# The expert phase of an attention, MLP and mixture-of-experts kernel: lists loaded at a tile's begin, weights asked for behind the branch on the count, raw buffers refilled behind each conversion

## The chip, the cores and the metric

The kernel runs on one core of a Trainium2 chip. The metric is the device time of one execution in microseconds (us), as the median of several runs. A core has five engines that run their own instruction streams: TensorE (PE, matrix products), VectorE (DVE), ScalarE (ACT), GpSimd (POOL) and SyncE (SP, which here only asks for DMA transfers). They meet through semaphores.

## The reference, cut to what matters

```python
def _moe2_ref(x, w_gate, w1, w2):            # x: 2304 x 512, from attention and an MLP ahead of it
    logits = x @ w_gate                      # 8 experts
    expert_idx = np.argmax(logits, axis=1)
    probs = softmax(logits)
    gate_w = probs[np.arange(N), expert_idx]
    for e in range(E):
        mask = expert_idx == e
        if not mask.any():
            continue
        xe = x[mask]
        h = np.maximum(xe @ w1[e], 0.0)      # 512 -> 1024
        ye = h @ w2[e]                       # 1024 -> 512
        out[mask] = gate_w[mask, None] * ye
```

Attention (4 batches, 8 heads, 576 positions of 64) gives x, an MLP with 2048 hidden units follows, and then this expert phase. How many tokens an expert gets is known only when the gate has been computed. With the inputs shown the experts, sorted by size, have 1366, 515, 296, 103 and 24 tokens; the other three have none.

## The kernel before, in words

Attention and the MLP run to about 640 us of the span; a planner orders their instructions, and the change leaves that part alone. The expert phase (`run`, from L1185 on) takes the experts in order of size, r = 0, 1, 2, ... For each of them the tokens' numbers and gate weights stand in a list in DRAM (`info`, two 32-bit words for each token).

**Tiles.** An expert's tokens are cut into tiles of 256 (`tile256`), and what is left runs as a tile of 128 or 64 (`tile128`, `tile64`, in `remainder`); an expert with 128 tokens or fewer has only such a tile (`only`). So expert 0 has five tiles of 256 and one of 128, expert 1 two and one of 64, expert 2 one and one of 64, expert 3 one of 128, expert 4 one of 64. Tile j of expert r is called (r, j) here.

**Steps of a tile.** `fetch` loads the list of 256 tokens into `it` (a DMA of SP, L1020), copies it into `rem` for the remainder (L1024), and gathers the tokens' rows from DRAM into `xg`, in two halves of 128 rows (indirect DMAs of POOL, L1026). `xprep` transposes a half on TensorE (`Tx`, L1033); ScalarE and VectorE split it into a high and a low part (`cxh` L1035, `cxl` L1036). Then come two layers of three-pass products (L1060; L1143 in `tile64`), and a scatter of the scaled rows to the output (POOL, L1064).

**Weights.** The 16 weight blocks of an expert (256 KB each) are loaded by SP into 16 `raw` buffers (`wload`, L1004), and each is then split by `conv` (ScalarE L1014, VectorE L1015) into the tiles `e` that TensorE reads. The conversions of expert r+1 are `jobs`, handed out by `step` between the products of a tile of expert r; `ahead` holds the steps that prepare the next tile. `load_next`, called behind a tile that has conversions, asks for the blocks of expert r+2 in the 16 buffers.

**Branches.** All five engines follow the branches on the counts. `few0` (L1295) and `many0` (L1302) branch on the size of expert 0, `less{r}` (L1313) and `more{r}` (L1317) on that of expert r; L1316 leaves the loop when nothing is left (in the trace it has the line of the loop's frame, L1307). `hint` (L1199) marks a place where an engine is told which way a labelled branch will go, so that the instructions there can be fetched ahead. An engine that jumps over a part adds what that part would have added to its semaphores; the trace has this as EVENT_SEMAPHORE and, for POOL, INC_SWDGE_SEM at the branch's line.

**Order around the change.** Tile (0, 0) runs ahead of the branch `few0`. Its `ahead` (L1286) holds, in this order, the counts, the 16 loads for expert 1, and the two transposes of tile (0, 1), whose gather is issued in the same tile. SP issues in program order, so what stands behind the 16 loads on its stream comes later.

Of the kernel before, what the change touches and what calls it, by code (L numbers as in the profile page):

```python
# [10 lines left out]
I32 = mybir.dt.int32  # L11
# [945 lines left out]
class Experts:  # L957
# [7 lines left out]
    def __init__(A, tc, K, wp, cp, psp, x2, info, w1, w2, out):  # L965
# [5 lines left out]
        A.its = [[cp.tile([P, 2, 2], I32, name=f"it{z}{q}") for q in range(2)] for z in range(2)]  # L971
# [8 lines left out]
    def itile(A, r, j):  # L980
        return A.its[0][r % 2] if j == 0 else A.its[1][j % 2]
# [35 lines left out]
    def fetch(A, r, j, base, rows=NT + 1):  # L1017
# [5 lines left out]
        if j:  # L1023
            A.nc.sync.dma_start(A.rem, src)  # L1024
        for h in range(2):
            A.nc.gpsimd.indirect_dma_start(out=A.xg[:, h], out_offset=None, in_=A.x2[0:rows, :], in_offset=IOA(ap=it[:, h, 0:1], axis=0))  # L1026
# [13 lines left out]
    def body(A, r, j, size, jobs=(), ahead=(), at={}, it=None, cond=None):  # L1040
# [13 lines left out]
        {2 * P: A.tile256, P: A.tile128, 64: A.tile64}[size](name, A.Ws[r % 2], A.itile(r, j) if it is None else it, A.xtile(j), step)  # L1054
# [40 lines left out]
    def tile128(A, n, W, it, x, step):  # L1095
# [22 lines left out]
        step(5)  # L1118
        l1(0, range(4))
        step(3)  # L1120
        l1(1, (0, 1))
        turn(0)
        step(2)
# [4 lines left out]
        step(7, 2)  # L1128
# [4 lines left out]
    def tile64(A, n, W, it, x, step):  # L1133
# [23 lines left out]
        def l2(h, fs):  # L1157
# [5 lines left out]
            if f == 7:  # L1163
                nc.scalar.mul(yo[0:64, c], Y[h][64:128], it[64:128, 0, 1:2].bitcast(F32))
                nc.vector.scalar_tensor_tensor(yo[0:64, c], Y[h][0:64], it[0:64, 0, 1:2].bitcast(F32), yo[0:64, c], op0=ALU.mult, op1=ALU.add)

        nc.sync.dma_start(it[64:128, 0], it[0:64, 0])
# [17 lines left out]
    def run(A, base, last, order, order_all):  # L1185
# [15 lines left out]
        def nexts(r, j, b, nb):  # L1201
            fs = [lambda: None] + xpreps(r, j) if b is not None else []
            if nb is not None:
                fs += [lambda: A.fetch(r + 1, 0, nb)]
                fs += [lambda: None] * (6 - len(fs)) + xpreps(r + 1, 0)
            return fs

        def load_next(r):
            if r < E - 2:
                A.load_raws(r + 2, reg(0, r + 2, E - 1))  # L1210

        def big(r, j, b, jobs=(), nb=None):
# [4 lines left out]
            if more:  # L1217
                A.fetch(r, j + 1, b)
            A.body(r, j, 2 * P, jobs, nexts(r, j + 1, b if more else None, nb))
            if jobs:  # L1220
                load_next(r)
# [31 lines left out]

        def only(r, nb):

            jobs = [lambda: A.fetch(r + 1, 0, nb)] + [lambda i=i: A.conv(r + 1, i) for i in range(16)] if r < E - 1 else []
            if r < E - 2:
                jobs[-1] = lambda: (A.conv(r + 1, 15), load_next(r))

            def go(size):  # L1260
                hint(f"more{r}", ns[r] > P)
                A.body(r, 0, size, jobs, xpreps(r + 1, 0) if jobs else (), cond=ns[r + 1] > 0 if jobs else None)

            with A.tc.If(ns[r] <= 64) as c:  # L1264
# [21 lines left out]
        ahead = [lambda: None] * 2 + [counts, lambda: A.load_raws(1, hold["e1"]), lambda: None] + xpreps(0, 1)  # L1286
# [230 lines left out]
```

## Time and profile before

| | |
|---|---|
| median of 3 runs | 927.5 us (924.5, 927.5, 933.88) |
| the profiled execution | 926.22 us, span 924.5 us |
| PE busy | 869.6 us (94% of the span) |
| DVE, ACT, POOL busy | 560.1, 401.7, 314.3 us |
| mean granted TensorE clock | 0.987 of full speed |

TensorE is busy nearly throughout. The idle time before an instruction is shown in a row with what ended it: an engine's instruction, a DMA, or an engine's sequencer (a name with q, as DVEq: a branch or a semaphore event of that stream). "issue" is time for which the profile shows no releaser. The rows that the prediction uses stand in a section of their own below.

### The profile page before, as it was taken

The page shows a single profiled execution, that of the slowest core. Times are in us where ns is not written, and L with a number is a line of the kernel's source. Part 1 is how long each engine was busy: PE and PEld are TensorE (multiplying, and loading weights), DVE is VectorE, ACT ScalarE, POOL GpSimd, SP SyncE. Part 2 cuts the span into 40 slices and gives each one's busy share as a digit, 9 for nine tenths or more (in the row PEclk, how much of TensorE's full clock was granted, in tenths as well). Part 3 has the DMA queues.
Part 4 walks back from the last instruction along what each step waited for, and adds up shares of the span by engine and source line. Part 5 has one row for each costly group of instructions (what it writes and reads, how often), then busy time and mean ns, then how long its engine had stood idle before and what let it go on. Part 6 is the DMA issues. An engine that isn't in the chain of part 4 may idle for free. (4 is left out here: it accounts for less than half of the span.)

```text
span 924.5 us, 17837 instructions
## 1 busy us (share of the span) xinstructions
PE 869.6 (94%) x6185; PEld 740.4 (80%) x6185; DVE 560.1 (61%) x1387; ACT 401.7 (43%) x1022; POOL 314.3 (34%) x332
## 2 busy tenths in 40 slices
PE   7998989999999999999999999999899998998883
PEld 6665657888888888888889989899788987888763
DVE  4999986757677767877756666556226211613450
ACT  6777765545445545555422121223225222523451
POOL 1555665433344354453342232341212111111110
PEclk9999989999999999999999999999999999999997
DMA  9982101323232133312111131153527212612561
GB/s 336 357 303 93 40 6 36 90 64 95 101 94 96 57 101 102 111 35 74 59 54 69 62 76 52 41 124 106 187 78 229 70 48 62 212 50 83 174 192 38
DMA packets 49724, 98.39 MB, mean 106 GB/s; under 512 B 12575, under 2 KB 19375, under 8 KB 49584
## 3 DMA queue, kind: packets, MB, share of 16 engines
q1 hardware_dynamic: 38720, 76.78, 25.6%
q0 software_dynamic: 4240, 11.56, 4.0%
q10 hardware_dynamic: 6624, 8.39, 2.6%
q8 instruction: 63, 1.03, 0.5%
q14 instruction: 77, 0.63, 0.2%
HBM read 83.43 MB, written 13.67 MB: 105 GB/s over the span
## 5 line engine op out<-in xcount | busy, mean ns | idle before, releaser
L707 PE MATMUL l<-xh,wi 128*128 128x256 f32 x1024 | 205.4, 285 | 1.4 <-DVE t L686 1.4
L707 PEld LDWEIGHTS l<-xh,wi 128*128 128x128 f32 x1024 | 166.7, 190 | 6.1 <-DVE t L686 1.8
L737 PE MATMUL acc<-wo,gh 128*128 128x512 f32 x512 | 166.0, 405 | 0.0
L707 PE MATMUL l<-xl,wi 128*128 128x256 f32 x512 | 144.6, 282 | 0.0
L713 POOL TENSOR_TENSOR gl<-t,gh 128x256 fp32r<-128x256 f32 x107 | 82.0, 766 | 180.3 <-ACT gh L710 149.7
L530 POOL TENSOR_SCALAR P<-P,sm 128x256 f32<-128x256 f32 (+4 forms) x71 | 88.3, 1250 | 101.5 <-ACT gh L710 46.5
L710 ACT CAST gh<-t 128x256 fp32r<-128x256 f32 x120 | 48.8, 406 | 170.2 <-DVE t L686 99.3
L685 DVE TENSOR_SCALAR t<-l,al 128x256 f32<-128x256 f32 x128 | 61.8, 483 | 86.9 <-PE l L707 84.8
L737 PE MATMUL acc<-wo,gl 128*128 128x512 f32 x256 | 100.5, 393 | 1.2 <-POOL gl L713 1.2
L707 PEld LDWEIGHTS l<-xl,wi 128*128 128x128 f32 x512 | 97.4, 190 | 3.8 <-issue 0.2
L737 PEld LDWEIGHTS acc<-wo,gh 128*128 128x128 f32 x512 | 86.6, 189 | 10.8 <-issue 0.5
L479 DVE TENSOR_REDUCE nb<-S 128x1 f32<-128x256 f32 (+4 forms) x160 | 69.5, 476 | 29.6 <-PE S L456 14.9
L524 ACT COPY F<-PT 128x384 f32<-128x384 f32 (+2 forms) x126 | 58.5, 479 | 64.2 <-PE PT L519 60.8
L823 DVE SCALAR_TENSOR_TENSOR xt<-y,xr_wg 128x512 f32<-128x512 f32 x96 | 73.8, 769 | 9.1 <-DMA xr_wg<-in_wgT_dram 5.2
L519 PE MATMUL PT<-ident,P 128*128 128x128 f32 (+1 forms) x400 | 64.9, 282 | 7.4 <-DVE xo L573 5.3
L496 ACT ACTIVATE P<-S,nb 128x128 f32<-128x128 f32 (+3 forms) x128 | 66.7, 529 | 9.3 <-DVE nb L479 8.5
L519 PEld LDWEIGHTS PT<-ident,P 128*128 128x128 f32 (+1 forms) x400 | 45.5, 140 | 21.1 <-DVE xo L573 5.0
L1060 PE MATMUL l<-cxh,e 128*128 128x256 f32 x320 | 58.2, 282 | 0.8 <-ACTq L1295 0.8
L737 PEld LDWEIGHTS acc<-wo,gl 128*128 128x128 f32 x256 | 48.1, 188 | 13.0 <-POOL gl L713 2.1
L686 DVE SCALAR_TENSOR_TENSOR t<-l,t 128x256 f32<-128x256 f32 x128 | 54.4, 425 | 4.4
L1060 PE MATMUL Y<-e,hh 128*128 128x512 f32 x176 | 56.2, 400 | 0.0
L1015 DVE TENSOR_TENSOR e<-raw,e 128x512 fp32r<-128x512 f32 x68 | 43.9, 685 | 19.5 <-ACT e L1014 19.3
(375 smaller groups left out, 1683.3 us busy)
## 6 DMA issues: line engine op xcount, KB each, us to landing
raw<-in_moe_w_dram SPq DMA_DIRECT2D x96, 256.0 KB, 4.2
xr_wg<-in_wgT_dram SPq DMA_DIRECT2D x24, 512.0 KB, 3.6
qk<-in_qk_dram SPq DMA_DIRECT2D x16, 608.0 KB, 3.9
rawi<-in_moe_w_in_dram SPq DMA_DIRECT2D x16, 512.0 KB, 8.8
rawo<-in_moe_w_out_dram SPq DMA_DIRECT2D x16, 512.0 KB, 10.6
v<-in_v_dram SPq DMA_DIRECT2D x16, 320.0 KB, 3.1
x<-y ACTq DMA_DIRECT2D x16, 256.0 KB, 3.3
xr<-xT SPq DMA_DIRECT2D x7, 512.0 KB
```

The costliest lines, as they stand in the source:

```text
L479: nc.vector.tensor_reduce(pl["nb", p, c][:, 2 * k + j:2 * k + j + 1], pl[Ss[j]][:, a:b], axis=AX.X, op=ALU.max, negate=True)
L496: nc.scalar.activation(pl[x][:, a:b], pl[Ss[j]][:, a:b], AF.Exp, bias=nb, scale=1.0, accum_out=pl["sm", p, c][:, 2 * k + j:2 * k + j + 1])
L519: nc.tensor.transpose(pl[t][0:w, k], pl[x][:, P * k:P * k + w], A.K.ident)
L524: f(pl[F][:, 0:n], pl[t][:, 0:n])
L530: (nc.gpsimd if on == "POOL" else nc.vector).tensor_scalar(y, y, pl["sm", p, c][:, k:k + 1], None, op0=ALU.mult)
L685: nc.vector.tensor_scalar(pl[out], x, 0.0, A.K.al[:, f:f + 1], op0=ALU.min, op1=ALU.mult)
L686: nc.vector.scalar_tensor_tensor(pl[out], x, 0.0, pl[out], op0=ALU.max, op1=ALU.add)
L707: nc.tensor.matmul(pl[l][:, 0:G], lhsT=a[:, c], rhs=b, start=k == 0 and j == 0, stop=k == 3 and j == 2)
L713: (nc.gpsimd if on == "POOL" else nc.vector).tensor_sub(pl[gl], pl[t], pl[gh].bitcast(F32))
L737: nc.tensor.matmul(pl[acc], lhsT=x[:, c], rhs=w, start=f == 0 and j == 0, stop=f == 15 and j == 2)
L823: A.nc.vector.scalar_tensor_tensor(t, A.y(i), 1.0, wg, op0=ALU.mult, op1=ALU.mult, accum_out=A.L()[:, i, e:e + 1])
L1060: A.nc.tensor.matmul(ps, lhsT=x[a], rhs=w[b], start=first and q == 0, stop=last and q == 2)
```

## The change

`fetch` is taken apart into `lists` (SP) and `gather` (POOL). In `big` and `only` the next expert's list is asked for at the tile's begin, and only its gather stays in `ahead` or `jobs`. The lists of tiles j > 0 have three buffers in place of two. `tile64` no longer copies the upper half of its list from the lower half in SBUF; `lists` loads these 64 entries from DRAM a second time into `twins`. The 16 loads for expert 1 move from tile (0, 0), ahead of the branch `few0`, to the begin of tile (0, 1), behind it. A raw buffer is asked for again right behind its conversion (`convs`), in place of `load_next` behind the tile. In `tile128` the jobs are handed out as 4, 1, 3, 9 in place of 5, 3, 2, 7. In `only` the hint for `more{r}` moves from the tile's begin to behind the last conversion, and a new hint, for the new label `on{r}` (the branch that leaves the loop), stands at the begin.

```diff
-        A.its = [[cp.tile([P, 2, 2], I32, name=f"it{z}{q}") for q in range(2)] for z in range(2)]
+        A.its = [[cp.tile([P, 2, 2], I32, name=f"it{z}{q}") for q in range(2 + z)] for z in range(2)]
+        A.twins = cp.tile([P, 3, 2], I32, name="twins")
...
-        return A.its[0][r % 2] if j == 0 else A.its[1][j % 2]
+        return A.its[0][r % 2] if j == 0 else A.its[1][j % 3]
...
-    def fetch(A, r, j, base, rows=NT + 1):
+    def fetch(A, r, j, base):
+        A.lists(r, j, base)
+        A.gather(r, j)
+
+    def lists(A, r, j, base):
...
         if j:
             A.nc.sync.dma_start(A.rem, src)
+        if r or j:
+            A.nc.sync.dma_start(A.twins[64:128, 2 if j else r % 2], A.info[ds(base + 2 * P * j, 64), :])
+
+    def gather(A, r, j):
+        it = A.itile(r, j)
         for h in range(2):
...
-        step(5)
+        step(4)
         l1(0, range(4))
-        step(3)
+        step(1)
         l1(1, (0, 1))
         turn(0)
-        step(2)
+        step(3)
...
-        step(7, 2)
+        step(9, 2)
...
-    def tile64(A, n, W, it, x, step):
+    def tile64(A, n, W, it, x, step, twin):
...
-                nc.scalar.mul(yo[0:64, c], Y[h][64:128], it[64:128, 0, 1:2].bitcast(F32))
+                nc.scalar.mul(yo[0:64, c], Y[h][64:128], twin[64:128, 1:2].bitcast(F32))
...
-        nc.sync.dma_start(it[64:128, 0], it[0:64, 0])
...
             if nb is not None:
-                fs += [lambda: A.fetch(r + 1, 0, nb)]
+                fs += [lambda: A.gather(r + 1, 0)]
...
-        def load_next(r):
-            if r < E - 2:
-                A.load_raws(r + 2, reg(0, r + 2, E - 1))
-
-        def big(r, j, b, jobs=(), nb=None):
+        def big(r, j, b, jobs=(), nb=None, raws=None):
...
             if more:
                 A.fetch(r, j + 1, b)
+            if nb is not None:
+                A.lists(r + 1, 0, nb)
+            if raws is not None:
+                A.load_raws(1, raws)
             A.body(r, j, 2 * P, jobs, nexts(r, j + 1, b if more else None, nb))
-            if jobs:
-                load_next(r)
...
+        def convs(r):
+
+            e = reg(0, r + 1, E - 1) if r < E - 1 else None
+
+            def one(i):
+                A.conv(r, i)
+                if e is not None:
+                    A.wload(r + 1, e, i, A.raws[i])
+
+            return [lambda i=i: one(i) for i in range(16)]
+
         def only(r, nb):
 
-            jobs = [lambda: A.fetch(r + 1, 0, nb)] + [lambda i=i: A.conv(r + 1, i) for i in range(16)] if r < E - 1 else []
-            if r < E - 2:
-                jobs[-1] = lambda: (A.conv(r + 1, 15), load_next(r))
+            jobs = [lambda: A.gather(r + 1, 0)] + convs(r + 1) if r < E - 1 else []
+            if jobs:
+                jobs[-1] = lambda f=jobs[-1]: (f(), hint(f"more{r}", ns[r] > P))
 
             def go(size):
-                hint(f"more{r}", ns[r] > P)
+                hint(f"on{r}" if jobs else f"more{r}", ns[r + 1] > 0 if jobs else ns[r] > P)
...
+            if jobs:
+                A.lists(r + 1, 0, nb)
...
-        ahead = [lambda: None] * 2 + [counts, lambda: A.load_raws(1, hold["e1"]), lambda: None] + xpreps(0, 1)
+        ahead = [lambda: None] * 2 + [counts] + [lambda: None] * 2 + xpreps(0, 1)
...
         with A.tc.If(n0 > 5 * P, label="many0"):
-            big(0, 1, base)
+            big(0, 1, base, raws=hold["e1"])
             big(0, 2, base, convs(1), nb)
             bigs(0, 3, base)
...
-                    st.enter_context(A.tc.If(ns[r] + P * ns[r + 1] > P))
+                    st.enter_context(A.tc.If(ns[r] + P * ns[r + 1] > P, label=f"on{r}"))
```

The instructions of attention, the MLP and TensorE stand as before on every engine. Two places of the order follow.

SP around the branch `few0`, before (L1276 reads the counts into registers; `raw` are the weight blocks of expert 1, `it` and `rem` the list of tile (0, 2)):

```order
L1276 TENSOR_LOAD odri
L1276 ISA x16
L1199 REGISTER_ALU
L1512 BRANCH_PREFETCH_HINT
L1004 ISA
L1004 DMA raw_6145<-in_moe_w_dram 128x512
...
L1004 DMA raw_7980<-in_moe_w_dram 128x512
L1295 COMPARE_AND_BRANCH
...
L1302 COMPARE_AND_BRANCH
...
L1020 DMA it_6127<-info 128x2x2
...
L1024 DMA rem<-info 128x2x2
```

The same place with the change:

```order
L1300 TENSOR_LOAD odri
L1300 ISA x16
L1212 REGISTER_ALU
L1532 BRANCH_PREFETCH_HINT
L1316 COMPARE_AND_BRANCH
...
L1323 COMPARE_AND_BRANCH
...
L1026 DMA it_6129<-info 128x2x2
...
L1030 DMA rem<-info 128x2x2
...
L1032 DMA twins<-info 64x2
...
L1005 DMA raw_6147<-in_moe_w_dram 128x512
```

The 16 loads stood between the counts and the branch; they now stand behind both branches and behind the three loads of the list of tile (0, 2).

VectorE in the tile of 128 of expert 3, before, from its first hidden transpose on (`hl`: low part of a hidden transpose; `cxl`, `cxh`: the transposed rows of expert 4; `e`: converted weights of expert 4):

```order
L1112 TENSOR_TENSOR hl_6138<-Th_0_128+_0_14670,hh_6137 128x512
L1049 COMPARE_AND_BRANCH
L1015 TENSOR_TENSOR e_7_7882<-raw_7972,e_7_7882 128x512
L1015 TENSOR_TENSOR e_8_7902<-raw_7973,e_8_7902 128x512
L1049 UNCONDITIONAL_BRANCH x2
L1112 TENSOR_TENSOR hl_6140<-Th_0_128+_1_14696,hh_6139 128x512
L1049 COMPARE_AND_BRANCH
L1036 TENSOR_TENSOR cxl_6134<-Tx_0_0_14704,cxh_6133 128x4x128
L1038 TENSOR_TENSOR cxh_6133<-Tx_0_0_14704,cxh_6133 128x4x64
L1036 TENSOR_TENSOR cxl_6134<-Tx_0_1_14712,cxh_6133 128x4x128
L1015 TENSOR_TENSOR e_9_7937<-raw_7974,e_9_7937 128x512
...
L1015 TENSOR_TENSOR e_15_8213<-raw_7980,e_15_8213 128x512
```

The same with the change, from the second hidden transpose on:

```order
L1126 TENSOR_TENSOR hl_6142<-Th_0_128+_1_14808,hh_6141 128x512
L1060 COMPARE_AND_BRANCH
L1047 TENSOR_TENSOR cxl_6136<-Tx_0_0_14816,cxh_6135 128x4x128
L1049 TENSOR_TENSOR cxh_6135<-Tx_0_0_14816,cxh_6135 128x4x64
L1047 TENSOR_TENSOR cxl_6136<-Tx_0_1_14824,cxh_6135 128x4x128
L1016 TENSOR_TENSOR e_7_7884<-raw_7974,e_7_7884 128x512
L1016 TENSOR_TENSOR e_8_7904<-raw_7975,e_8_7904 128x512
...
L1016 TENSOR_TENSOR e_15_8216<-raw_7982,e_15_8216 128x512
L1212 REGISTER_ALU
L1532 BRANCH_PREFETCH_HINT
```

The conversions 7 and 8 moved from ahead of the second hidden transpose to behind the rows of expert 4, so that nine stand there in place of seven, and the hint for `more3` stands behind the last of them.

## Rows read from the trace of the kernel before

**Rows 1.** Busy time by stretch: start:end, length, busy PE, PEld, DVE, ACT, POOL; clock; DMA

```profile
640.00:912.00 272.00, 248.88 (x1589) 220.44 (x1588) 97.25 (x189) 94.65 (x181) 46.46 (x47) 0.99 0.38 120
```

**Rows 2.** What TensorE waited for in the expert phase: total us, times, longest

```profile
PE Tx L1033 <- DMA xg<-x,it: 4.0, 3, 2.3
PE l_256+_0_13337 L1060 <- DVEq L1313: 3.8, 1, 3.8
PE l_256+_0_11049 L1060 <- ACTq L1313: 2.9, 1, 2.9
...
PE Tx L1033 <- issue: 2.7, 1, 2.7
PE H_64+_0_15726 L1143 <- DVEq L1049: 1.3, 1, 1.3
```

**Rows 3.** Timeline of PE: start, us, instruction; in brackets the idle time before

```profile
663.29 0.63 PE L1033 MATMUL Tx<-ident,xg 128*128 128x128 f32 x4 [2.25 <-DMA xg<-x,it]
...
681.53 0.63 PE L1033 MATMUL Tx<-ident,xg 128*128 128x128 f32 x4 [1.06 <-DMA xg<-x,it]
```

**Rows 4.** Timeline of POOL, gathers (xg) and one scatter (out_dram) of tile (0, 0)

```profile
656.86 0.96 POOL L1026 DMA_INDIRECT xg<-x,it  x1 [0.30 <-issue]
...
666.32 1.00 POOL L1064 DMA_INDIRECT out_dram<-yo,it  x1 [7.16 <-ACTq L1295]
677.96 0.98 POOL L1026 DMA_INDIRECT xg<-x,it  x1 [10.63 <-PE l L1060]
...
885.12 0.97 POOL L1026 DMA_INDIRECT xg<-x,it  x1 [0.30 <-issue]
```

**Rows 5.** Timeline of SP's DMA issues: expert 1's weights, the list of (0, 2)

```profile
657.11 11.53 SPq L1004 DMA_DIRECT2D raw<-in_moe_w_dram  x16
675.36 0.39 SPq L1020 DMA_DIRECT2D it<-info  x1
```

**Rows 6.** DMA issues from 640 to 700: KB each, median us to landing

```profile
it<-info SPq DMA_DIRECT2D x4, 2.0 KB, 1.8
```

**Rows 7.** Line 1295 (branch few0) on SP: duration ns, first and last start

```profile
L1295 SPq EVENT_SEMAPHORE  x9: 17/17/17, 670.9 to 674.9; - x9
...
L1295 SPq COMPARE_BRANCH  x1: 87/87/87, 668.7 to 668.7; - x1
```

**Rows 8.** Timeline of ACT: the first conversion of expert 1

```profile
691.67 0.61 ACT L1014 CAST e<-raw 128x512 fp32r<-128x512 f32 x1
```

**Rows 9.** Timeline of PE: rows of expert 4, and its tile's first product

```profile
892.80 0.63 PE L1033 MATMUL Tx<-ident,xg 128*128 128x128 f32 x4 [2.74 <-issue]
...
900.44 0.74 PE L1143 MATMUL H_64+_0_15726<-e,cxh 128*128 128x256 f32 x4 [1.26 <-DVEq L1049]
```

**Rows 10.** Timeline of DVE in expert 3's tile: last transposed rows, then conversions

```profile
894.08 0.69 DVE L1036 TENSOR_TENSOR cxl<-Tx,cxh 128x512 fp32r<-128x512 f32 x1 [2.31 <-ACT cxh L1035]
894.69 4.29 DVE L1015 TENSOR_TENSOR e<-raw,e 128x512 fp32r<-128x512 f32 x7
```

**Rows 11.** Line 1313 (branch less2) on DVE, 836 to 843

```profile
L1313 DVEq COMPARE_BRANCH  x1: 75/75/75, 839.5 to 839.5; - x1
...
L1313 DVEq EVENT_SEMAPHORE  x1: 21/21/21, 841.8 to 841.8; - x1
```

**Rows 12.** Line 1317 (branch more3) on DVE, 893 to 906

```profile
L1317 DVEq COMPARE_BRANCH  x1: 81/81/81, 898.7 to 898.7; - x1
...
L1317 DVEq EVENT_SEMAPHORE  x1: 21/21/21, 899.4 to 899.4; - x1
```

**Rows 13.** Line 1307 (branches that leave the loop) on POOL, 912 to 925

```profile
L1307 POOLq EVENT_SEMAPHORE  x4: 17/42/43, 916.1 to 916.4; - x4
...
L1307 POOLq COMPARE_BRANCH  x2: 60/80/99, 913.0 to 918.0; - x2
...
L1307 POOLq INC_SWDGE_SEM  x1: 1470/1470/1470, 916.5 to 916.5; - x1
```

**Rows 14.** The kernel's last line on POOL, 912 to 925

```profile
L1512 POOLq DRAIN  x3: 51/109/5377, 918.2 to 924.2; - x3
```

More of the change, by code (lines that the diff above doesn't have):

```diff
@@ L1024, in fetch @@
             A.nc.sync.dma_start(A.rem, src)
+        if r or j:
+            A.nc.sync.dma_start(A.twins[64:128, 2 if j else r % 2], A.info[ds(base + 2 * P * j, 64), :])
+    def gather(A, r, j):
+        it = A.itile(r, j)
         for h in range(2):
-            A.nc.gpsimd.indirect_dma_start(out=A.xg[:, h], out_offset=None, in_=A.x2[0:rows, :], in_offset=IOA(ap=it[:, h, 0:1], axis=0))
+            A.nc.gpsimd.indirect_dma_start(out=A.xg[:, h], out_offset=None, in_=A.x2[0:NT + 1, :], in_offset=IOA(ap=it[:, h, 0:1], axis=0))
     def xprep(A, r, j, h):
@@ L1053, in body @@
         name = f"{r}_{j}_{size}{'+' if jobs else ''}"
-        {2 * P: A.tile256, P: A.tile128, 64: A.tile64}[size](name, A.Ws[r % 2], A.itile(r, j) if it is None else it, A.xtile(j), step)
+        args = [name, A.Ws[r % 2], A.itile(r, j) if it is None else it, A.xtile(j), step]
+        if size == 64:
+            args.append(A.twins[:, r % 2 if it is None else 2])
+        {2 * P: A.tile256, P: A.tile128, 64: A.tile64}[size](*args)
         assert not jobs and not ahead
@@ L1290, in run @@
         n0 = ns[0]
-        def convs(r):
-            return [lambda i=i: A.conv(r, i) for i in range(16)]
         with A.tc.If(n0 <= 5 * P, label="few0"):
             with A.tc.If(n0 > 3 * P) as c:
-                big(0, 1, base, convs(1), nb)
+                big(0, 1, base, convs(1), nb, hold["e1"])
             with c.Else():
-                for f in [lambda: A.fetch(1, 0, nb)] + convs(1) + xpreps(1, 0) + [lambda: load_next(0)]:
+                for f in [lambda: A.fetch(1, 0, nb), lambda: A.load_raws(1, hold["e1"])] + convs(1) + xpreps(1, 0):
                     f()
@@ L1311, in run @@
                 nb = reg(2, r + 1, (E - 1) * NT) if r < E - 1 else None
-                jobs = convs(r + 1) if r < E - 1 else []
                 with A.tc.If(ns[r] <= P, label=f"less{r}"):
@@ L1315, in run @@
                 if r < E - 1:
-                    st.enter_context(A.tc.If(ns[r] + P * ns[r + 1] > P))
+                    st.enter_context(A.tc.If(ns[r] + P * ns[r + 1] > P, label=f"on{r}"))
                 with A.tc.If(ns[r] > P, label=f"more{r}"):
-                    big(r, 0, base, jobs, nb)
+                    big(r, 0, base, convs(r + 1) if r < E - 1 else [], nb)
                     bigs(r, 1, base)
```

## Prediction

> **What bounds the kernel now.** I read the page's busy times first, then busy time by stretch, what TensorE waited for, and the timelines around its longest waits. Everything that the change touches lies behind 640 us. There TensorE is busy 248.88 of 272.00 us [rows 1], and its instructions stay the same in number and order, so the change can move only the 23.1 us in which TensorE is idle there, and the tail behind its last product. The list of waits [rows 2] splits the largest part of that: 4.0 us for gathered rows (`xg`), 3.8 and 2.9 us at two passages of line 1313, 2.7 us without a releaser, 1.3 us for VectorE at the start of expert 4's tile. The rest is in small pieces that no edit touches. So the gain is bounded by some microseconds of 927, well under 1%.
>
> **The gather of tile (0, 1).** Its second half is issued at 656.86 [rows 4], the first of 16 weight loads at 657.11 [rows 5]; TensorE reads the half at 663.29 after 2.25 idle [rows 3], so it was wanted at 663.29 − 2.25 = 661.04 and came 6.4 us after its issue. Without the weights such a gather takes less: the one issued at 677.96 [rows 4] is read at 681.53 [rows 3], 3.6 us. In the changed kernel SP reaches the branch where it reached the weights, at 657.1. The jump cost SP 670.9 − 668.7 = 2.2 us before [rows 7], and three short list loads stand next, each about 0.6, estimated from the issue time of one (0.39 [rows 5]) and a like gap. The weights then start near 657.1 + 2.2 + 1.8 = 661.1, when the half has landed (656.86 + 3.6 = 660.5). **−2.25 us**; if the gather is not slow through the weights, 0.
>
> **The gather of tile (0, 2).** SP reaches this tile's list at 675.36 [rows 5], because behind the branch it waits for the weights in flight: nine semaphore events from 670.9 to 674.9 [rows 7]. The list lands 1.8 us after its issue [rows 6], and the gather is issued at 677.96 [rows 4], late by 1.06 us at TensorE [rows 3]. With the change nothing is in flight there, and the list is asked for near 659.5. POOL then waits only for its own stream: the last scatter of tile (0, 0) at 666.32 [rows 4], 2.25 earlier now, and what POOL adds to semaphores behind it. So the gather is issued near 665.5, and wanted at 681.53 − 1.06 − 2.25 = 678.2: a margin of 12.7 us. It runs under the weights now. The slowest gather under weights in these rows, issued at 885.12 [rows 4] and read at 892.80 [rows 9], took 7.7 us, so it is in time. **−1.05 us** (0 to −1.06). The Trainium skill, "DMA: Bandwidth & Descriptors", section "Issuing engines are not separate DMA queues", has transfers asked for by SP and by POOL run on the same 16 DMA engines and interleave. By that the change would only move the collision from one gather to the next; the gather of 7.7 us agrees that they collide, and the margin of 12.7 us decides that nobody waits for it.
>
> **Later weights.** The loads for expert 1 end about 5 us later than before (661.1 + 11.53 = 672.6, and some us to land). Their first reader starts at 691.67 [rows 8]. **0**; without these 13 us and more of cover, each microsecond of delay would be one of ScalarE's, which sets the pace of nothing there.
>
> **Tile of 128, expert 3.** The gather of expert 4 is the tile's first job. Behind it 5 + 3 + 2 − 1 = 9 conversions run ahead of the transposes, each of which frees a buffer for a load of 256 KB; now 4 + 1 + 3 − 1 = 7. The second half took 7.7 us against 3.6 free of weights, 4.1 more, 0.46 for each of nine loads. Two fewer: 2 × 0.46 = **−0.9 us** of the 2.74 that TensorE waited [rows 9]. The ends are 0 (the loads left over are enough to delay it) and −2.74 (the half is in time). I take the share because loads and gather draw on one supply.
>
> Against it stand two more conversions on VectorE behind the second half's rows. VectorE did seven there in 4.29 us [rows 10], 0.61 each, from 894.69 on, and then expert 4's first product at 900.44 had waited 1.26 us for it [rows 9]. VectorE is what is late at that place, so nine cost 2 × 0.61 = **+1.2 us**. What bounds this from below is 0 (then ScalarE or the branch would have to be late instead), and from above 1.2, since the two are 0.61 each.
>
> **The hint for `more3`** stood at the tile's begin and now stands behind the last conversion, just ahead of its branch. Before, VectorE passed that branch in 899.4 − 898.7 = 0.7 us [rows 12]; line 1313 at 839.5 took 841.8 − 839.5 = 2.3 [rows 11]. [...] The ends are 0 and 2.3 − 0.7 = 1.6; I take **+0.6 us**, nearer to the short one because the hint still comes first.
>
> **The exit.** POOL ran from a branch at 913.0 to events at 916.1, then 1.47 us of adding to semaphores [rows 13], then a drain of 5.38 [rows 14]. The new hint for `on4` may take the 3.1 us of the first, but these events also wait for the last scatter to land, and that takes the same microseconds. **−0.5 us**, between 0 and −1.1.
>
> **At nothing.** The lists' third buffer and the earlier list loads take waits from SP, and gathers that TensorE does not wait for hide them. The copy for `tile64`, and the 512 bytes of `twins` in its place, are small DMAs far ahead of their readers. The refill behind each conversion does not move the loads: before, SP had passed on to them and waited for each conversion in turn. The read of the expert's number for it is a few hundred nanoseconds on SP, which is idle. The cover of all these is SP's idle time; should it go, each list would come later by 0.6.
>
> **Sum.** −2.25 − 1.05 − 0.9 + 1.2 + 0.6 − 0.5 = −2.9. On the profiled 926.22 us that is 923.3. The median of the runs shown, 927.5, stands 1.3 above the profiled execution, so I forecast 923.3 + 1.3 = 924.6, that is **924.5 us**. The kernel's own runs spread over 9 us; about 1% (9.3 us) is what its measurement can tell from no change.
>
> **Rivals.**
>
> *The weights collide all the same.* The jump at `few0` is quicker than 2.2 us, or the half takes its 6.4 us for another reason, or the gather of (0, 2) waits for something besides its list (its row names a product of TensorE as the releaser). Then the first two terms give 0 to 1 of 3.3 us, and the rest of the sum is +0.4: 926 to 927 on the profiled, **928** on the median. For it: the first half, ahead of the weights, had TensorE waiting too (three waits make the 4.0 [rows 2]). Against it: 2.25 is the wait of the half beside the weights alone. Chance 0.14.
>
> *Passages become cheap.* New code and new hints lie otherwise, and the two waits at line 1313, 3.8 and 2.9 us [rows 2], lose the 2.3 us of a far jump each [rows 11]: 924.6 − 4.6 = **920**; with expert 4's gather wholly in time (−1.8 more) 918. Against it: no hint for `less` was touched. Chance 0.13.
>
> *Passages become dear: the slower case.* Each branch lies now in front of other code, and the streams have grown by hints and loads. If two passages that were near become far on the engine that TensorE waits for, at 2.3 us each, and the hint for `more3` comes too late altogether (1.6 in place of 0.6), the sum is −2.9 + 4.6 + 1.0 = +2.7: 929 on the profiled, **930** on the median. It decides from two such jumps on; one leaves the sum near 0. For it: line 1313 shows that a hint given a tile ahead does not save every jump. The Trainium skill, "Runtime: NRT & Kernel Launch", section "Instruction fetch mechanics", says that a taken branch whose target isn't in the window of fetched instructions forces a fetch before the engine goes on. The 2.3 against 0.7 us of the two rows agree with it, and by it any shift of code can go either way. Chance 0.15.
>
> **Chances and range.** Forecast 0.58, the three rivals 0.14, 0.13, 0.15. The forecast's own ends: with all bounds good, −2.25 − 1.05 − 2.74 + 0 + 0 − 1.1 = −7.1, or 920.4; with all bad, the first two gone in part, near 928. The range takes in these and most of the rivals: **918 to 930**. Faster by over 1% (under 918.2) needs cheap passages and all bounds good, or a draw of the runs: 0.10. Slower by over 1% (over 936.8) needs four or five new far jumps: 0.05. Within 1%: 0.85.
>
> **What would show it.** In the new trace the row for `xg` in TensorE's waits falls from 4.0 to about 0.7; SP asks for the list of (0, 2) near 659.5 and for the first weights near 661; the transposes of expert 4's second half wait about 1.8 instead of 2.74; the first product of expert 4 still waits for VectorE, now behind nine conversions. The gather of (0, 2) takes 6 to 8 us and nobody waits for it. The prediction is wrong if SP's weights start ahead of 660, if TensorE waits for converted weights of expert 1, or if the waits at lines 1313, 1317 and their new numbers change by over 2 us.

## The result and the profile after

| | before | changed |
|---|---|---|
| median | 930.74 us (20 runs, 924.5 to 941.03) | 922.77 us (20 runs, 917.86 to 929.79) |
| ratio | 1 | 0.9914 (0.9893 to 0.9936) |
| profiled execution | 926.22 us, span 924.5 | 919.38 us, span 917.6 |
| TensorE idle from 640 us to its last product | 22.6 us | 18.0 us |

The change saves 8.0 us (6.0 to 10.0). The forecast was 2.9 us less than before, as 924.5 us in a range of 918 to 930; the measured time lies in the range, and the gain is nearly three times the forecast. The forecast's own anchor, the profiled execution and three runs, was a low draw: with 20 runs the kernel before has a median 3.2 us above the 927.5 shown then. So it is luck that the measured time comes within 1.7 us of 924.5: an anchor 3.2 us too low and a gain 5.1 us too small cancel in part.

The first view is busy time by stretch in the changed kernel, up to its last product (start:end, length, busy PE, PEld, DVE, ACT, POOL, clock, DMA). It answers to [rows 1].

```profile
640.00:904.52 264.52, 246.51 (x1590) 219.28 (x1589) 97.38 (x189) 94.34 (x180) 46.62 (x47) 0.99 0.40 124
```

Length minus busy PE is the idle time: 18.0 us. The same view of the kernel before, to its last product at 911.49, gives 271.49 − 248.88 = 22.6. Idle time is 4.6 us less; products took 2.4 us less. Up to 1.7 us of that is the clock, by estimate: one stretch of 3.4 us at half clock stands there where the kernel before had two. From this pair of profiles alone that part can't be put down to the change; the repeated profiles below have four such stretches in either kernel.

What TensorE waited for in the changed kernel (total us, times, longest), beside [rows 2]:

```profile
PE H L1157 <- issue: 3.7, 1, 3.7
PE Tx L1044 <- issue: 3.0, 2, 2.6
PE l_256+_0_13441 L1074 <- ACTq L1333: 2.7, 1, 2.7
PE l_256+_0_11126 L1074 <- PEq L1333: 2.1, 1, 2.1
...
PE H_64+_0_15854 L1157 <- ACTq L1337: 1.3, 1, 1.3
```

The row for `xg`, 4.0 us before, is gone. The two waits at the `less` branches (line 1313, now 1333) went from 2.9 and 3.8 to 2.1 and 2.7. The wait for expert 4's rows (`Tx <- issue`) went from 2.7 to 3.0, and the one ahead of expert 4's tile stays at 1.3. The first row is the entry into expert 2's tile of 64, 2.9 before.

SP's issues around `few0` (start, us, issue), the events of the branch on SP and POOL's adding there, and POOL's issues, beside [rows 5], [rows 7] and [rows 4]:

```profile
664.13 0.39 SPq L1026 DMA_DIRECT2D it<-info  x1
...
666.67 12.41 SPq L1005 DMA_DIRECT2D raw<-in_moe_w_dram  x16
```

```profile
L1316 SPq EVENT_SEMAPHORE  x9: 17/17/17, 660.4 to 661.0; - x9
...
L1316 SPq COMPARE_BRANCH  x1: 83/83/83, 657.7 to 657.7; - x1
...
L1316 POOLq INC_SWDGE_SEM  x1: 672/672/672, 663.4 to 663.4; - x1
```

```profile
656.10 0.96 POOL L1037 DMA_INDIRECT xg<-x,it  x1 [0.30 <-issue]
...
663.19 1.00 POOL L1078 DMA_INDIRECT out_dram<-yo,it  x1 [4.79 <-ACTq L1316]
666.97 0.98 POOL L1037 DMA_INDIRECT xg<-x,it  x1 [2.77 <-DMA it<-info]
```

TensorE's reading of the second half of tile (0, 1) and of the first of (0, 2), beside [rows 3]:

```profile
660.20 0.60 PE L1044 MATMUL Tx<-ident,xg 128*128 128x128 f32 x4
...
677.27 0.60 PE L1044 MATMUL Tx<-ident,xg 128*128 128x128 f32 x4
```

No bracket of idle time stands at either. The half issued at 656.10 is read 4.1 us later, against 6.4 under the weights. SP passes the branch from 657.7 to 661.0, where it waited for the weights until 674.9 before. Its list is out at 664.13 all the same, not at 659.5 as forecast: ahead of it SP waited 2.7 us, until 664.0, and that is where POOL's adding to its semaphores at `few0` ends, behind the scatter of 663.19. (The list of SP's waits names the gather for `xg` instead, but TensorE had read those rows at 660.20. In the second profile of the change and in the move alone, below, the list is out 0.9 to 1.0 us behind that scatter's start too.) The weights so begin at 666.67, 5.6 us later than forecast; nobody waits for them, nor for the gather issued at 666.97, which has ten microseconds.

### The profile page after: what moved, and what is told of

Same layout as the page of the kernel before. It is cut to its first block, busy times and chain, and to the rows that moved or that the text cites. A ratio compares the mean times of both kernels' runs of the same rounds, so it can differ in the third digit from the quotient of the medians.

```text
span 917.6 us, 17890 instructions
## 1 busy us (share of the span) xinstructions
PE 868.6 (95%) x6185; PEld 740.8 (81%) x6185; DVE 560.5 (61%) x1387; ACT 402.0 (44%) x1022; POOL 314.6 (34%) x332
## 5 line engine op out<-in xcount | busy, mean ns | idle before, releaser
L479 DVE TENSOR_REDUCE nb<-S 128x1 f32<-128x256 f32 (+4 forms) x160 | 69.5, 475 | 29.5 <-PE S L456 14.7
L519 PEld LDWEIGHTS PT<-ident,P 128*128 128x128 f32 (+1 forms) x400 | 45.6, 141 | 19.6 <-DVE xo L573 3.4
L1078 POOL DMA_INDIRECT out_dram<-yo,it x18 | 18.1, 1007 | 118.7 <-ACT yo L1106 66.2
```

Source lines behind the costliest of these rows:

```text
L479: nc.vector.tensor_reduce(pl["nb", p, c][:, 2 * k + j:2 * k + j + 1], pl[Ss[j]][:, a:b], axis=AX.X, op=ALU.max, negate=True)
L519: nc.tensor.transpose(pl[t][0:w, k], pl[x][:, P * k:P * k + w], A.K.ident)
```

## The experiments

"Idle" is TensorE's idle time from 640 us to its last product, length minus busy time of the view above; the tail behind that product is not in it. Ratios are to the kernel before.

| kernel | ratio (95%) | idle us |
|---|---|---|
| before, two profiles | 1 | 22.6, 24.5 |
| change, two profiles | 0.9914 (0.9893 to 0.9936), 0.9920 (0.9892 to 0.9949) | 18.0, 17.5 |
| move alone, two profiles | 0.9947 (0.9926 to 0.9969), 0.9957 (0.9931 to 0.9984) | 19.6, 20.2 |
| change without the move | 1.0001 (0.9976 to 1.0027) | 22.8 |
| change without its hints | 0.9915 (0.9890 to 0.9939) | 20.4 |
| change with jobs 5, 3, 2, 7 | 0.9917 (0.9888 to 0.9946) | 18.5 |
| change, loads held | 0.9898 (0.9861 to 0.9936) | 15.8 |
| change, loads held, jobs 5, 3, 2, 7 | 0.9923 (0.9900 to 0.9946) | 16.5 |
| change with a hint for the remainder | 0.9922 (0.9898 to 0.9947) | 20.2 |
| change with filling products | 0.9899 (0.9879 to 0.9919) | 15.2 |
| held, 5, 3, 2, 7, and filled | 0.9904 (0.9883 to 0.9926) | 14.7 |

**The change without the move of the 16 loads.**

```diff
-        ahead = [lambda: None] * 2 + [counts] + [lambda: None] * 2 + xpreps(0, 1)
+        ahead = [lambda: None] * 2 + [counts, lambda: A.load_raws(1, hold["e1"]), lambda: None] + xpreps(0, 1)
...
-            big(0, 1, base, raws=hold["e1"])
+            big(0, 1, base)
```

> The changed kernel with the 16 loads for expert 1 back in tile (0, 0), ahead of the branch few0; all else stays. Theory A (the loads delayed three halves of two gathers, 4.0 us in all; the other 3 us of the gain have another cause): the three waits for xg come back, 0.7 + 2.3 + 1.1, and the kernel takes about 4 us more than the change: ratio to the kernel before 0.9957, PE's last product near 908.5. The waits at the less branches stay at about 2.0 and 2.7. Rival B (freeing SP early is what shortens the later branches too): all of the gain goes, ratio 1.000. Rival C (the lists, asked for at the tile's begin, are what helps, since the third wait came from a late list): only 3 of the 4 us come back, the gather of (0, 2) stays in time, ratio 0.995.

Measured 1.0001: the whole gain goes. TensorE's waits, and SP's issues:

```profile
PE Tx L1044 <- DMA xg<-x,it: 4.9, 2, 4.0
...
PE l_256+_0_11094 L1074 <- ACTq L1333: 2.9, 1, 2.9
PE l_256+_0_13409 L1074 <- ACTq L1333: 2.8, 1, 2.8
```

```profile
659.84 10.94 SPq L1005 DMA_DIRECT2D raw<-in_moe_w_dram  x16
...
677.29 0.40 SPq L1026 DMA_DIRECT2D it<-info  x1
```

The `xg` row is back, as theory A had it, but 4.0 us of it are one wait now, for the gather of (0, 2): the second half of (0, 1) came in time here, the weights having started 1.8 us behind its issue in place of 0.25 us, and so TensorE came earlier to a gather whose list was still behind the weights. That refutes rival C: a list asked for at a tile's begin helps nothing while 16 loads stand ahead of the branch. The number is rival B's, not theory A's 0.9957: half of the loss isn't in the `xg` waits. This profile had its products at half clock in five places behind 640 us, the change's first in one. The timed runs bear that out in part: their mean granted clock is 0.980 in 12 runs here, 0.981 in the 28 runs of the kernel before beside them, and 0.983 in 30 runs of the change; by estimate, 0.003 of 917 us, nearly 3 us of the loss are the clock. And ScalarE's jump at `less1` takes 2.1 us again, where it takes 0.5 in the change, though only SP's loads were moved.

**The move alone**, in the kernel before, run twice.

```diff
+            if raws is not None:
+                A.load_raws(1, raws)
             A.body(r, j, 2 * P, jobs, nexts(r, j + 1, b if more else None, nb))
...
-            big(0, 1, base)
+            big(0, 1, base, raws=hold["e1"])
```

> The kernel before with one edit: the 16 loads for expert 1 behind the branch few0, behind the list of tile (0, 2). Theory A: the three waits for xg go, the rest stays as before: 4.0 us less, ratio 0.9957; the waits at the less branches stay at 2.9 and 3.8, with the half clock behind the second. Rival B: the whole gain, ratio 0.9914 or about 8 us, with the waits at the less branches at 2.0 and 2.7.

> The kernel before with only the 16 loads moved behind few0, once more, beside the unedited change in the same call. Theory (the move is the whole gain; the other edits cancel): ratio to the kernel before within 0.002 of that of the change in this call, about 0.993. Rival (the other edits give 3 us of their own, as the first comparison of 0.9947 with 0.9914 has it): 0.003 or more above the change.

Measured 0.9947 and 0.9957, 4.0 to 5.0 us, as theory A had it. From its first profile:

```profile
PE l_256+_0_13369 L1060 <- DVEq L1315: 3.8, 1, 3.8
PE l_256+_0_11081 L1060 <- ACTq L1315: 3.2, 1, 3.2
...
PE Tx L1033 <- DMA xg<-x,it: 1.0, 1, 1.0
```

Two of the three `xg` waits are gone, the waits at the `less` branches are those of the kernel before. Both times the ratio is 0.0033 to 0.0037 above that of the change, which is the rival's side of the second expectation. The second time the two kernels were timed side by side: 12 runs of the move have a mean of 927.6 us, ten of the change 924.4, a difference of 3.2 (1.2 to 5.2), at nearly the same mean clock (0.982 in both). So the other edits together do give some 3 us, once the move is made; which of them does was not tried.

**The change without its hints.** The hint for `more` stands at the begin again, hint and label `on` are out.

```diff
-                jobs[-1] = lambda f=jobs[-1]: (f(), hint(f"more{r}", ns[r] > P))
...
-                hint(f"on{r}" if jobs else f"more{r}", ns[r + 1] > 0 if jobs else ns[r] > P)
+                hint(f"more{r}", ns[r] > P)
...
```

> The changed kernel with the hint for more back at the tile's begin, and without the hint and label on. Theory A with hints (the two hints move every later instruction of ACT and DVE by a few places, and by that the jumps at less1 on ACT and less2 on DVE found their target near): ACT's jump at less1 takes 2.1 us again and DVE's at less2 2.3, the waits are 2.9 and 3.8 again, the half clock behind the second comes back (1.4 us): 3.3 us more than the change, ratio 0.995. Rival (the jumps are cheap for another reason, as SP's freedom or chance of the run): no difference from the change, ratio 0.9914. PE's jump at more3 takes 0.4 instead of 2.2 us either way, which nobody waits for.

Measured 0.9915, the rival's number. VectorE at `less2`, first in the change, then in this kernel, against 839.5 to 841.8 before [rows 11]:

```profile
L1333 ACTq COMPARE_BRANCH  x1: 60/60/60, 833.7 to 833.7; - x1
L1333 DVEq COMPARE_BRANCH  x1: 75/75/75, 834.2 to 834.2; - x1
...
L1333 DVEq EVENT_SEMAPHORE  x1: 21/21/21, 834.8 to 834.8; - x1
...
L1333 ACTq EVENT_SEMAPHORE  x1: 17/17/17, 835.7 to 835.7; - x1
```

```profile
L1331 DVEq COMPARE_BRANCH  x1: 75/75/75, 834.6 to 834.6; - x1
...
L1331 DVEq EVENT_SEMAPHORE  x1: 21/21/21, 835.2 to 835.2; - x1
```

VectorE's passage takes 0.6 us in both, so the hints didn't make it short, and my theory on them falls. ScalarE's own passage, 2.0 us, is last now, which is why a jump shorter by 1.7 gives only 1.0 of the wait. That short passage, 0.58 to 0.59 us, stands in nine profiles of kernels with the change's other edits, and 2.3 to 2.5 us in the four without (and in one with them, the hint for the remainder below); which of them does it (lists, `twins`, refill) was not tried one by one and stays open. The late hint for `more3` costs something on TensorE's own stream, as expected of this run: with the hint back at the tile's begin the branch takes under 0.5 us; in the change it takes 2.2:

```profile
L1337 PEldq COMPARE_BRANCH  x1: 2151/2151/2151, 886.8 to 886.8; - x1
```

It ends at 889.0, while products run until 892.05: off the path.

**The change with the jobs of the tile of 128 at 5, 3, 2, 7.**

```diff
-        step(4)
+        step(5)
         l1(0, range(4))
-        step(1)
+        step(3)
...
```

> The changed kernel with the jobs of the tile of 128 handed out as 5, 3, 2, 7 again. Theory (two terms cancel: two raw loads more ahead of the gather of expert 4 make its second half later by about 0.9, two conversions fewer behind it give 1.2 back): between 0 and -0.5 us against the change, ratio 0.9909 to 0.9914. Rival (the order of the jobs gave part of the gain): 1 us or more slower than the change, ratio 0.9925 or above.

Measured 0.9917: no difference that can be told, as the theory had it.

```profile
PE Tx L1044 <- issue: 2.4, 2, 1.9
PE H_64+_0_15854 L1157 <- DVEq L1337: 1.8, 1, 1.8
```

The waits move against my terms: the gather's is 0.6 shorter than in the change with two raw loads more ahead of it, and the one at expert 4's tile 0.5 longer with two conversions fewer behind. A wait also depends on when TensorE arrives. From the rows' transposes to the tile's first product it is 902.28 − 895.33 = 6.95 us here and 8.0 in both profiles of the change, so the two conversions do cost 1.0 us. TensorE, with no stretch at half clock on the way here, was through with expert 3 sooner, and so the wait comes out longer.

**The change once more.**

> The changed kernel once more, unedited, to see what stays from execution to execution. The waits for xg stay away; the wait at less1 (2.05 in its first profile, 2.90 and 2.92 in two kernels whose TensorE, ScalarE and VectorE code is the same or nearly so) may come out at either; the stretches at half clock lie elsewhere or are of another number. Ratio 0.990 to 0.9935. If the theory is wrong that jumps and clock differ by execution, waits and half-clock stretches come out as in the first profile, within 0.1 us.

Measured 0.9920. Waits and one stretch of this profile (clock is the third column from the end):

```profile
PE l_256+_0_13441 L1074 <- ACTq L1333: 3.0, 1, 3.0
...
PE l_256+_0_11126 L1074 <- PEq L1333: 2.1, 1, 2.1
...
PE Tx L1044 <- DMA xg<-x,it: 0.9, 1, 0.9
```

```profile
838.00:844.00 6.00, 5.70 (x26) 5.71 (x27) 0.69 (x1) 0.74 (x2) 2.36 (x2) 0.50 0.35 67
```

The wait at `less1` repeats, and so does ScalarE's jump there, 0.48 us in both profiles: I had left open whether it goes by the execution, and it doesn't. The first half of (0, 1) costs 0.9 here and nothing in the first profile: so the 0.7 that I had left standing does stay as a rule (a wait of 0.6 to 1.1 for `xg` stands in every other kernel with the move). And behind a wait of 3.0 us at `less2` TensorE runs at 1.2 GHz, where behind 2.7 us in the first profile it ran at 2.4:

```profile
838.00:842.00 4.00, 4.00 (x36) 4.00 (x35) 1.89 (x3) 1.79 (x4) 1.64 (x2) 1.00 0.55 94
```

**The kernel before once more.**

> The kernel before once more, unedited. Its first profile had 6.8 us at half clock behind 640 us, the changed kernel's two profiles 3.4 and 17. If the clock differs by execution, this profile has the same waits for xg (4.0 us in all, within 0.5) and another number of half-clock stretches than 6.8 us. If the kernel before always has 6.8, the clock is no lottery, and its waits draw fewer stretches than those of the change.

```profile
PE l_256+_0_13337 L1060 <- DVEq L1313: 3.9, 1, 3.9
PE Tx L1033 <- DMA xg<-x,it: 3.6, 3, 2.0
```

The waits repeat (3.6 for `xg`, 3.9 and 2.8 at `less`), and so do the jumps behind them (VectorE at `less2` 2.3 and 2.5 us, ScalarE at `less1` 2.1 and 2.0). But stretches at half clock stand in four places behind 640 us in place of two; in the change it was one and four. The clock differs by execution in both kernels, and four profiles show no difference between them in it. The timed runs show a small one: the mean granted clock is 0.9815 over 65 runs of the kernel before (0.975 to 0.988) and 0.9832 over 30 of the change (0.976 to 0.991), which is 1.6 us by estimate, at the edge of the noise.

**Loads held.** For an expert with only a small tile, the first eight buffers are asked for again behind the ninth; the second run holds nine and goes back to 5, 3, 2, 7.

```diff
-                if e is not None:
-                    A.wload(r + 1, e, i, A.raws[i])
+                if e is not None and i >= hold:
+                    for k in [i] + (list(range(hold)) if i == hold else []):
+                        A.wload(r + 1, e, k, A.raws[k])
...
-            jobs = [lambda: A.gather(r + 1, 0)] + convs(r + 1) if r < E - 1 else []
+            jobs = [lambda: A.gather(r + 1, 0)] + convs(r + 1, 8) if r < E - 1 else []
```

> The changed kernel, with the first eight raw buffers of an expert that has only a small tile asked for again behind the ninth, so that SP holds these loads until the gathered rows have been transposed. It decides two things. If the raw loads are what delays the gather of expert 4, TensorE's waits of 0.4 and 2.6 us for it go (under 0.3 left in all), 3 us less than the change; if that wait also draws the half clock behind it (3.4 us at half speed, 1.7 us of loss), 4 to 5 us less, ratio to the kernel before 0.9865 to 0.988. If the gather is slow by itself or waits for its list, the waits stay and the ratio is 0.9914.

> The changed kernel with the loads of an expert that has only a small tile held until its tenth conversion, and the jobs of the tile of 128 at 5, 3, 2, 7. Holding the loads alone left TensorE 0.7 us for the gather in place of 2.9, but 2.8 in place of 1.3 for VectorE at expert 4's tile. Theory (VectorE's last conversions are what is late next): two conversions fewer behind the rows, the wait for VectorE falls by 1.2 to about 1.6, the gather stays at 0.7 or less: 2.5 us less than the change, ratio 0.989. Rival (the two earlier conversions delay the hidden transposes by as much): the waits only move, ratio 0.990 to 0.9915.

Measured 0.9898 (0.9861 to 0.9936) and 0.9923 (0.9900 to 0.9946): neither told from the change. Waits of the two:

```profile
PE H_64+_0_15852 L1157 <- DVEq L1338: 2.8, 1, 2.8
...
PE Tx L1044 <- PE Tx L1044: 0.7, 1, 0.7
```

```profile
PE H_64+_0_15852 L1157 <- DVEq L1338: 1.8, 1, 1.8
...
PE Tx L1044 <- PE Tx L1044: 0.2, 1, 0.2
```

The mechanism is shown: without loads in flight the rows of expert 4 cost TensorE 0.7 and 0.2 in place of 2.9 to 3.0. Half of it comes back as a wait for VectorE's conversions, 2.8 in place of 1.3; with two conversions fewer behind the rows 1.8, as expected (1.6). Idle time falls by 1.5 to 2 us, but the timed runs don't show it, and the traces say why: SP now jumps at `more3` with the held loads still in flight, its adding there ends at 911.1 (899.9 in the change), and ScalarE's last scaling waits for it. First in the change, then with the loads held:

```profile
903.16 0.47 ACT L1178 ACTIVATE yo<-Y_64+_0_15929,twins 64x256 f32<-64x256 f32 x1 [1.52 <-PE Y_64+_0_15929 L1176]
```

```profile
911.12 0.47 ACT L1178 ACTIVATE yo<-Y_64+_0_15921,twins 64x256 f32<-64x256 f32 x1 [5.55 <-SPq L1338]
```

From TensorE's last product to the end it is 15.6 and 15.1 us with the loads held (15.2 in the third such kernel, below) against 13.1 and 13.3 in the change. The 2 us saved ahead are paid back in the tail. (One more profile has a tail of 15.6, the second of the move alone, so a tail can also differ by execution.)

**A hint for the branch on the remainder's size**, which has none in either kernel.

```diff
+            if r and A.TOP[r] > 2 * P + 64:
+                fs += [lambda: None] * (4 - len(fs))
+                f = fs[3]
+                fs[3] = lambda: (f(), hint(f"odd{r}", ((ns[r] + (P - 1)) & (2 * P - 1)) > P - 1 + 64))
...
-                with A.tc.If(left(64)) as c:
+                with A.tc.If(left(64), label=label) as c:
```

> The changed kernel with a hint, in the middle of each tile of 256 of experts 1 to 7, for the branch that tells a remainder of 128 from one of 64 (it has none in either kernel). If TensorE's jump there is slow because nothing fetched its target, the 2.6 us that its branch took at 860.8 fall to about 0.5, the wait ahead of expert 2's tile of 64 from 3.7 to some 2.5 (ACT and VectorE bound it then), 1 us less or more with the clock: ratio 0.990. If only one hint is held, the hint for rest given earlier is lost, and the branch of rest becomes slow in its place: same time or up to 2 us more, ratio 0.9914 to 0.9935.

Measured 0.9922, no difference. TensorE's branch ahead of expert 2's tile of 64, in the change and in this kernel, and what this kernel pays elsewhere:

```profile
L1247 PEldq COMPARE_BRANCH  x1: 2612/2612/2612, 860.8 to 860.8; - x1
```

```profile
L1247 PEldq COMPARE_BRANCH  x1: 82/82/82, 867.5 to 867.5; - x1
```

```profile
PE l_256+_0_13701 L1074 <- DVEq L1337: 4.2, 1, 4.2
PE H_64+_0_16319 L1157 <- DVEq L1341: 3.4, 1, 3.4
...
PE Th_128+_0_15157 L1123 <- ACT yo L1118: 2.0, 1, 2.0
```

The jump fell from 2.6 us to 0.1, and the wait behind it from 3.7 to 2.1, with ACT and VectorE last as expected. But VectorE's passage at `less2` is long again (2.4 us, as in the kernel before, with a wait of 4.2), a new wait of 2.0 stands in expert 3's tile, and expert 4's tile waits 3.4 for VectorE in place of 1.3. The other side of the expectation came in too, at one place: TensorE's branch of `rest` took 3.4 us at 818.7 in place of 0.4, while its products ran on. Idle time comes out at 20.2 us, 2 above the change.

**Filling products** that nobody reads: nine behind expert 1's last product, eight between the gathered halves of expert 4; and the first alone on top of the held loads.

```diff
+    def fill(A, r, name, n):
+        t, W = A.psp.tile("T", f"fill{name}", (P, 512)), A.Ws[r % 2]
+        for k in range(n):
+            A.nc.tensor.matmul(t, lhsT=W[0][0][:, 0:P], rhs=W[1][0], start=True, stop=True)
...
```

> The changed kernel with products whose result nobody reads: nine of 128x512 behind the last product of expert 1, where TensorE waits 2.7 to 3.0 us at less2, and eight between the two gathered halves of expert 4, where it waits 2.6. They take about 2 us each time. Theory (a wait costs its own time and, in most executions, also a stretch of 3.4 or 6.8 us at half clock behind it): the same waits in sum, shorter pieces, and no half clock behind these two places; 2 to 3 us less than the change, ratio to the kernel before 0.989. Rival (the clock does not go by these waits, or falls elsewhere instead): same time as the change, 0.9915; if the filling products come too late to stand in the wait, 2 to 4 us more, 0.994 to 0.996.

> Both: late_steps, and nine products that nobody reads behind the last product of expert 1. If the two gains are real and apart, 0.987 to 0.988, the fastest of all; if the clock falls in other places instead, as late_steps.

Measured 0.9899 and 0.9904, where 0.989 and 0.987 to 0.988 were expected. From the first:

```profile
PE H_64+_0_15892 L1162 <- DVEq L1347: 3.2, 1, 3.2
...
PE l_256+_0_13461 L1074 <- ACTq L1343: 1.0, 1, 1.0
```

```profile
836.00:840.00 4.00, 3.33 (x28) 3.37 (x29) 0.69 (x1) 0.79 (x2) 1.61 (x2) 1.00 0.07 4
```

The wait at `less2` is 1.0 us long, and the stretch behind it runs at 2.4 GHz in both filled kernels; it did not in four of the seven other profiles with the change's code there, which two profiles alone don't set apart from chance. The timed runs do show that filling keeps the clock up: it is 0.986 to 0.990 in all six runs of the first, with a mean of 0.989, against 0.983 for the change. By estimate that is worth 5 us (0.0055 of 917), of which less than half shows in the time, since the filling takes TensorE time of its own. Between the halves the filling only moved TensorE's wait to VectorE (3.2). The two have, with the first of the held loads, the lowest ratios of all, but their intervals overlap the change's: no version is shown to beat it.

## Why the prediction was right in its direction and too small

Point by point, with the mean of two profiles of each kernel:

| step | forecast us | measured us |
|---|---|---|
| second half of (0, 1), first of (0, 2) | −3.3 | −3.1 (2.25 + 1.06, 1.97 + 0.90 to 0, 0) |
| first half of (0, 1) | 0 | −0.2 (0.7, 0.7 to 0, 0.9) |
| gather of expert 4 | −0.9 | 0.0 (2.7, 3.2 to 3.0, 2.9) |
| two conversions behind the rows | +1.2 | 0.0 in the wait (1.3 to 1.3), +0.3 from rows to tile |
| late hint for `more3` | +0.6 | 0.0 (VectorE's passage 0.6 to 0.6; TensorE's branch 0.4 to 2.2, hidden) |
| exit | −0.5 | +0.3 (13.0, 12.9 to 13.1, 13.3) |
| passages at `less1`, `less2` | 0 | −0.8, −1.0 |

**What carried the sum held.** The gain of 3.3 us from the gathers is right in place and size, shown by the move alone (0.9947, 0.9957) and by its undoing (1.0001). The chain was right that SP, waiting behind the branch for loads in flight, was what held the list; it missed that SP then waits until POOL's adding at the same branch is through.

**The step that failed is the one put at nothing by silence: the passages at line 1313.** The forecast left them as they were and gave their change to a rival at 0.13. They fell by 1.8 us in sum, just under the 2 us that the prediction had named as a sign of being wrong. At `less2` this is steady: VectorE's jump takes 0.6 in place of 2.3 us. At `less1` it hangs on the program: ScalarE's jump takes 0.48 us in both profiles of the change and 0.45 to 0.48 in four other kernels with its edits, and 2.0 to 2.1 in four more (the one without the move, and all three with jobs 5, 3, 2, 7). Why the code's place decides it stays open.

**The two costs did not reach TensorE as priced.** VectorE's nine conversions take 5.5 us now, in its timeline, beside [rows 10]:

```profile
887.21 5.50 DVE L1016 TENSOR_TENSOR e<-raw,e 128x512 fp32r<-128x512 f32 x9
```

and TensorE's last wait for expert 4's rows, and its wait at the tile, beside [rows 9]:

```profile
885.32 0.63 PE L1044 MATMUL Tx<-ident,xg 128*128 128x128 f32 x4 [2.62 <-issue]
...
893.31 1.18 PE L1157 MATMUL H_64+_0_15854<-e,cxh 128*128 128x256 f32 x8 [1.26 <-ACTq L1337]
```

From the rows' transposes to the tile's first product it was 900.44 − 892.80 = 7.64 us before and is 893.31 − 885.32 = 7.99 now: 0.35 more, not 1.2. The reading that VectorE was what was late there was wrong for this profile. Its seven conversions ended at 894.69 + 4.29 = 898.98, and TensorE's last product for expert 3, in the kernel before, at 899.18:

```profile
898.78 0.40 PE L1060 MATMUL Y_128+_14689<-e,hl 128*128 128x512 f32 x1
```

So the 1.26 us that followed were the engines' way through the branches, and two conversions more first used up what VectorE had to spare. It had that because TensorE ran at half clock for 3.4 us of this stretch, in both profiles of both kernels. Where no half clock lies in it, the stretch takes 6.7 to 7.0 us with seven conversions (four profiles) and 8.0 with nine (two; 8.7 in the kernel with the hint for the remainder): 1.0 us or more, about the price put on them.

No run shows the +0.6 us for the late hint: VectorE passes `more3` from 892.5 to 893.1 now, as long as the 0.6 to 0.7 of [rows 12], and what the late hint lengthened is TensorE's own branch, behind its products. The share of 0.46 us for each raw load did no better: two loads fewer ahead gave the half 0.4 us in all (7.3 us from issue in place of 7.7), and TensorE came that much sooner.

**The exit** did not get shorter: POOL's events there come 3.6 us behind the start of the last scatter (905.82 to 909.4), 3.3 before, and then comes the drain. The hint for `on` takes nothing off it: without the hints the tail is 12.9 us. POOL's events at the branch and the kernel's end, beside [rows 13] and [rows 14]:

```profile
L1328 POOLq EVENT_SEMAPHORE  x4: 17/43/43, 909.4 to 909.7; - x4
```

```profile
L1532 POOLq DRAIN  x3: 50/104/5385, 911.4 to 917.4; - x3
```

Last product to end: 924.5 − 911.49 = 13.0 before, 917.6 − 904.52 = 13.1 now.

**What is left.** Idle time fell by 5.8 us in the mean of two profiles (23.5 to 17.8), the timed runs by 7.5 to 8.0. The 2 us between lie inside the intervals, and the higher mean clock of the timed runs (1.6 us by estimate) would fill most of it. That the move alone gives 4 to 5, the rest alone nothing, and both 8 is only half explained: without the move the collision goes on to the next gather (4.9 us of `xg` waits), ScalarE's jump at `less1` is long again, and the clock is lower, so the rest can't show. The remainder stays open.

**Short and long jumps.** At the same branches the traces have passages of 0.1 to 0.6 us and of 1.5 to 4.1 us, and a hint half a tile ahead took TensorE's from 2.6 to 0.1. The Trainium skill, "Runtime: NRT & Kernel Launch", section "Instruction fetch mechanics", says that a taken branch whose target is outside the fetched window has to wait for a fetch. That there are two kinds of passage agrees with it, though no row here shows a fetch itself. The rival of dear passages had the sign wrong for the change: its shifted code made jumps shorter. The kernel with the hint for the remainder has one of them long again.

## What to carry to other kernels

In these kernels a queue that jumps over a part of the program first waits for the transfers that it has in flight (SP to 674.9 us before, to 661.0 with nothing in flight), so what it asks for ahead of a branch delays everything behind it; ask behind the branch, after the small list that a gather needs. The held loads show the same at the other end: asked for late, they made the last branch, and with it the kernel's tail, 2 us later. Before a cost is put on an engine that is late at some point, look which second engine is late by nearly as much, and price only what passes it. Where the waits left are jumps of 2 to 3 us, an edit's shift of the code can be worth as much as the edit itself: whether a jump of ScalarE or VectorE is short or long repeats from profile to profile of one program and can change with the next edit, while the clock does not repeat. So profile a kernel twice before a microsecond is explained, and read the granted clock of the timed runs too.

## What the runs showed of the hardware that was not expected

The same wait of 2 to 4 us is followed by a stretch of some 3.4 or 6.8 us at 1.2 GHz in one execution and not in another of the same program: behind `less2` after 3.0 us of idle time yes, after 2.7 us no. Nor does its length decide: after 2.8 us the clock fell there in the change without the move, and not in the one without its hints nor in the second with held loads. From 640 us to the last product the half clock covered 3.4 us in one profile of the change and 17 in the other. A late hint can be worse than an early one on the same branch: TensorE's `more3` took 0.4 us in each of five profiles with the hint at the tile's begin, and 1.5 to 4.1 in nine with the hint just ahead. And a jump at one place can change by 1.5 us with an edit to another engine's loads (ScalarE at `less1`, 0.5 and 2.1).
